# A chain of attention and two feed-forward layers: the second layer in three blocks of 768 tokens, its output product by Strassen's scheme too

## The chip, the core and the metric

The kernel runs on one core of one Trainium2 chip. The metric is the device time of one execution in microseconds (us); several executions are timed and their median is quoted.

## The reference, cut to what matters

```python
attn_out = _attn_ref(q, k, v, M_prev, z_prev, beta)        # B, H, S, D = 4, 8, 576, 64
x = attn_out.transpose(0, 2, 1, 3).reshape(2304, 512)
h = x @ w_in1;  r = np.maximum(h, 0.0)                     # 512 -> 2048
x = (s * (r * r) + b) @ w_out1                             # 2048 -> 512
h = x @ w_in2                                              # 512 -> 2048
sp = np.where(h > 20.0, h, np.log1p(np.exp(np.minimum(h, 20.0))))
out = (h * np.tanh(sp)) @ w_out2                           # 2048 -> 512
```

The weights arrive as 64-bit floats. The change is in the last three lines, "layer 2", and in how its weights are got ready.

## The kernel before

**Precision.** Every product is made of three fp32r products: an operand x is split into a high part (ScalarE copies it into an fp32r tile) and a low part (VectorE subtracts the high part from x), and high*high, low*high and high*low are added in PSUM. So each operand of a product costs a ScalarE copy and a VectorE subtraction, called a split below.

**Order.** The kernel is a list of steps with priorities. `Plan.order` runs them through a small model of the engines when the program is built and so fixes the order of the instructions on every engine; on the chip each engine runs its list in order, and semaphores hold back what isn't ready. A `Ring` is a set of buffer slots; `more(..., after=x)` adds slots that come free when step x is done.

**Layers.** Attention and layer 1 overlap. Layer 1 works on five blocks of 256 tokens and then two of 512 (`first`, `y_part`, `y_out`) and stores its result, transposed, in DRAM (`y_d`). Meanwhile `convert` turns the 64-bit weights into fp32: ScalarE, VectorE and one GpSimd addition (L656) for each of 32 pieces of 128x512 for layer 2, each then stored to DRAM (L670). The first pieces of layer 2 can go through once attention has left its buffers (`opened`).

**Layer 2.** Four blocks of 512 tokens and one of 256. `mish` makes one q of eight, that is 256 of the 2048 hidden columns: the input product is done by Strassen's scheme (in Winograd's form, seven products in place of eight) over two halves of the tokens, of the hidden columns and of the inner dimension; each product is six matmuls of 256 columns (L979). Three PSUM banks hold the results, VectorE adds them up (L985), ScalarE applies the activation (L989), and `finish` splits it (L935, L936). `load_y` makes the seven token-side operands of a block, `load_w` loads the weights of one q, forms their four sums on VectorE (L918) and splits them (L928, L929), anew for every block. `plain_pair` does the 256-token block without the scheme (L951). `o_part` is the output product in the plain form, 512 columns a matmul (L1014), put between the products of the next q. The split output weights stay in SBUF (`split_second`, once, L679 and L681). GpSimd has no work in layer 2.

## Time and profile before

| | |
|---|---|
| time, median of 3 runs | 1063.2 us (1062.54 to 1063.77) |
| the profiled execution, its own time | 1062.23 us |
| its span, first to last instruction | 1060.4 us |
| mean granted TensorE clock | 0.992 of full speed |
| attention with layer 1 | about 0 to 663 us of the span, its last products to 684 us |
| layer 2 | 663 to 1060 us |

PE is TensorE's matmuls, PEld its weight loads, DVE is VectorE, ACT ScalarE, POOL GpSimd; SPq is the queue from which SyncE issues DMAs. A matmul's bar is longer than its share of the time, since matmuls overlap; the pace is read from one start to the next.

### The profile page before, as it was taken

The numbers are of one execution on the slowest core, as the hardware profiler recorded it, in microseconds if no ns is written. First come the engines' busy times: TensorE is split into PE (matmuls) and PEld (weight loads), VectorE is DVE, ScalarE is ACT, GpSimd is POOL, SyncE is SP. The second block draws the span as 40 slices with busy tenths as digits, with TensorE's granted clock in tenths as the row PEclk, the third lists the DMA queues.
The fourth block names the chain that finished last, engine by engine and source line by source line (L and its number), as shares of the span: only waits on it lengthen the run. The fifth ranks groups of instructions, "written<-read, shape, count | busy, mean of one in ns | idle before, by whom it ended". The sixth has DMA issues, their size and how long they took to land.

```text
span 1060.4 us, 19441 instructions
## 1 busy us (share of the span) xinstructions
PE 1028.4 (97%) x6590; PEld 915.5 (86%) x6590; DVE 839.8 (79%) x2342; ACT 652.3 (62%) x1532; POOL 251.8 (24%) x337
## 2 busy tenths in 40 slices
PE   6989998999999999999989999999999999999998
PEld 4657787999999999999867888888899999999897
DVE  6899999999999999966797595796876977875432
ACT  6876897788888877865436553654453644553342
POOL 6854444343334334303224220000000000000000
PEclk9998998999999999999999999999999999999999
DMA  9663462323432423326546843331221221221220
GB/s 257 183 183 115 144 208 92 109 87 110 126 93 87 126 87 87 100 81 225 164 137 206 265 146 100 119 120 60 81 80 61 70 100 41 70 89 52 81 100 20
DMA packets 72051, 123.56 MB, mean 117 GB/s; under 512 B 7184, under 2 KB 48656, under 8 KB 71952
## 3 DMA queue, kind: packets, MB, share of 16 engines
q1 hardware_dynamic: 71520, 122.32, 37.5%
q8 instruction: 52, 0.85, 0.3%
q14 instruction: 47, 0.39, 0.1%
q10 hardware_dynamic: 432, 0.01, 0.0%
HBM read 99.75 MB, written 22.54 MB: 115 GB/s over the span
## 4 chain that ended last, share of the span: by engine, by line
PE 71%; DVE 14%; issue 4%; ACT 3%; DMA 3%; POOL 1%; DVEq 0%; ACTq 0%; POOLq 0%
PE o L1014 19%; PE h L723 12%; PE y L789 9%; PE h L979 9%; PE o L979 5%; PE a L567 4%; PE o L789 4%; PE a L539 3%; DVE total L693 2%; PE a L481 2%; PE h L951 1%; PE a L482 1%; DVE w L654 1%; PE o L723 1%; DVE Pt L486 1%
## 5 line engine op out<-in xcount | busy, mean ns | idle before, releaser
L656 POOL TENSOR_TENSOR w<-w,raw 128x512 int32<-128x512 int32 x54 | 75.7, 1402 | 166.9 <-DVE w L654 114.2
L498 POOL TENSOR_SCALAR Pt<-ex,nm 128x64 f32<-128x64 f32 x148 | 74.3, 515 | 85.4 <-PE a L539 45.7
L495 ACT ACTIVATE Pt<-Pt,mx 128x64 f32<-128x64 f32 (+4 forms) x148 | 81.8, 555 | 16.7 <-DVE mx L486 15.7
L539 PE MATMUL a<-ident,Pt 128*128 128x128 f32 x432 | 66.9, 281 | 9.1 <-POOL Pt L512 6.8
L547 DVE TENSOR_TENSOR PTl<-a,PTh 128x128 fp32r<-128x128 f32 (+1 forms) x144 | 64.0, 481 | 2.4 <-ACT PTh L544 1.6
L1014 PE MATMUL o<-woh,yh 128*128 128x512 f32 x232 | 63.4, 391 | 0.0
L1014 PE MATMUL o<-woh,gg 128*128 128x512 f32 x228 | 63.2, 394 | 0.0
L539 PEld LDWEIGHTS a<-ident,Pt 128*128 128x128 f32 x432 | 50.1, 143 | 14.5 <-POOL Pt L512 9.6
L486 DVE CUSTOM_DVE_ANT_0 Pt<-a,mask 128x320 f32<-128x320 f32 (+3 forms) x148 | 59.3, 417 | 3.3 <-PE a L482 1.5
L512 POOL TENSOR_SCALAR Pt<-Pt,rs 128x64 f32<-128x64 f32 x64 | 45.3, 755 | 64.3 <-DVE rs L517 50.9
L544 ACT CAST PTh<-a 128x128 fp32r<-128x128 f32 (+1 forms) x144 | 55.2, 431 | 3.3 <-PE a L539 2.4
L929 DVE TENSOR_TENSOR wil<-raw,wih 128x512 fp32r<-128x512 f32 (+2 forms) x69 | 52.3, 775 | 2.6 <-ACT wih L928 2.5
L789 PE MATMUL y<-gh,wol 128*128 128x256 f32 x320 | 54.0, 292 | 0.0
L789 PE MATMUL y<-gl,woh 128*128 128x256 f32 x320 | 53.5, 289 | 0.0
L789 PE MATMUL y<-gh,woh 128*128 128x256 f32 x320 | 53.0, 289 | 0.0
L989 ACT ACTIVATE g<-g 128x256 f32<-128x256 f32 (+1 forms) x42 | 21.9, 523 | 49.1 <-DVE g L985 48.9
L985 DVE TENSOR_TENSOR g<-o,g 128x256 f32<-128x256 f32 x58 | 24.5, 423 | 33.6 <-PE o L979 33.4
L567 PE MATMUL a<-PTl,V 128*128 128x384 f32 (+1 forms) x192 | 47.3, 293 | 1.6 <-DVE PTl L547 1.4
L567 PE MATMUL a<-PTh,V 128*128 128x384 f32 (+1 forms) x192 | 48.4, 280 | 0.0
L928 ACT CAST wih<-raw 128x512 fp32r<-128x512 f32 (+2 forms) x69 | 46.0, 687 | 2.7 <-DVE raw L918 1.3
L646 ACT ACTIVATE w<-raw 128x512 f32<-128x512 f32 x54 | 36.2, 671 | 17.4 <-DMA w_out_d<-w 8.8
L789 PEld LDWEIGHTS y<-gh,woh 128*128 128x128 f32 x320 | 45.4, 194 | 1.4 <-issue 0.7
(443 smaller groups left out, 3294.0 us busy)
## 6 DMA issues: line engine op xcount, KB each, us to landing
qk<-in_qk SPq DMA_DIRECT2D x24, 608.0 KB, 3.9
raw<-in_w_out SPq DMA_DIRECT2D x28, 512.0 KB, 3.9
raw<-w_in_d SPq DMA_DIRECT2D x28, 512.0 KB, 3.7
raw<-in_w_in SPq DMA_DIRECT2D x26, 512.0 KB, 4.6
wf<-w_in_d SPq DMA_DIRECT2D x12, 512.0 KB, 3.7
qn<-in_qz SPq DMA_DIRECT2D x29, 192.0 KB, 2.4
vx<-in_vm SPq DMA_DIRECT2D x29, 160.0 KB, 2.4
out<-ot SPq DMA_DIRECT2D x18, 256.0 KB, 2.1
```

Source lines behind the costliest of these rows:

```text
L486: nc.vector.tensor_tensor_reduce(Pt[t].t[:, D + lo:D + hi], ps.t[:, :hi - lo], mask[:, SP - w + lo:SP - w + hi], -SCALE, mx.t[:, t:t + 1] ...
L495: nc.scalar.activation(Pt[t].t[:, D:w + D], Pt[t].t[:, D:w + D], AF.Exp, bias=mx.t[:, t + i:t + i + 1], scale=-1.0, accum_out=rs.t[:, t:t ...
L498: add(POOL, 0.3, lambda: nc.gpsimd.tensor_scalar(Pt[t].t[:, :D], ex.t[:, t, :], nm.t[:, t:t + 1], 1.0, op0=ALU.mult, op1=ALU.mult), [ex, n ...
L539: nc.tensor.transpose(ps.t[:, c - c0, :], Pt[t].t[:, c * P:(c + 1) * P], ident)
L544: (nc.vector.tensor_copy if dve else nc.scalar.copy)(PT[0].t[:, at_], ps.t[:, :n])
L547: nc.vector.tensor_tensor(PT[1].t[:, at_], ps.t[:, :n], PT[0].t[:, at_].bitcast(F32), op=ALU.subtract)
L567: nc.tensor.matmul(o.rearrange("p (t q) -> p t q", q=P), v, x.t[:, f[0]:f[-1] + 1:f[1] - f[0] if len(f) > 1 else 1, :], start=(c == 0 and ...
L656: add(POOL, 1.23, prio, lambda: nc.gpsimd.tensor_tensor(w.t, w.t, words()[:, :, 0], op=ALU.add), [raw, low_words, w], [w])
L723: nc.tensor.matmul(ph, w_at(1, nm, r, cc)[:, o:o + P], x_at(x, cc), start=(part == 0 and cc == 0), stop=(part == 2 and cc == NCC - 1))
L789: nc.tensor.matmul(acc[ec // per].t[:, (ec % per) * n:(ec % per + 1) * n], w_at(1, nm, r, jj)[:, ec * P:(ec + 1) * P], t(x), start=(big an ...
L979: nc.tensor.matmul(ps.t[:, :h], w.t[:, i, kk], x.t[:, k, kk], start=begin and part == kk == 0, stop=part == 2 and kk == 1, skip_group_chec ...
L1014: nc.tensor.matmul(acc[i].t, gg.t[:, k, i * P:(i + 1) * P], W[2, nm, r][0].t[:, jj, :], start=(fc == 0 and part == 0), stop=(fc == NFC - 1 ...
```

## The change

Layer 2 takes three blocks of 768 tokens, all by Strassen's scheme. Each block runs in two phases. In the first (`hidden`, eight q), the input products are seven products of six matmuls with 384 columns; the four quarters of the activated result stay in SBUF as fp32 (`g2`), and VectorE forms three sums of them. In the second (`out_block`), the output product is done by the same scheme over halves of the tokens, the hidden columns and the output columns: seven products p of eight q, each 3 tiles of 128 tokens by 3 parts, in matmuls of 256 columns. Their token-side operands are split on the fly into a ring of eight slots (`S`), and VectorE adds the products into `p1`, `e2` and the output tile.

The sums of the weights are formed once, on GpSimd, while the weights are converted (`combine_in`, `combine_out`: four sums for each pair of pieces), and stored to DRAM with the pieces. Each block loads and splits the weights of each q and of each p anew. In the first block every second split weight tile (`kk`=1, `half`=1) is also stored split, and the later blocks load these tiles ready-made by a DMA issued from GpSimd's queue. The sums of the tokens' operands move from VectorE to GpSimd (`minus`), and so does one sum of the hidden quarters. PSUM is one pool of eight banks (`bk` in layer 2, three for a q or a p), and many buffers become parts of larger tiles (`Home`), whose homes are freed weights of layer 1. The ring `sc` for the sums and two more slots for converted pieces (`w32`) come free when layer 1's blocks of 256 tokens are done and stored (`small_left`).

```diff
-    N2 = 512
-    blocks2 = [(t, min(N2, NT - t)) for t in range(0, NT, N2)]
-    NB2 = len(blocks2)
+    N2 = 768
+    H2 = N2 // 2
+    NB2 = NT // N2
+    NQ2 = NFC // 2
+    DH = DM // 2
...
+    WID = [dram.tile([P, 2, 2, 7, P], F32, name=f"wi{r}_d") for r in range(NR)]
+    WOD = [dram.tile([P, 7, NQ2 // 2, DH], F32, name=f"wo{x}_d") for x in range(2)]
+    WIS = [dram.tile([P, 2, 7, P], F32R, name=f"wi_split{q}_d") for q in range(NQ2)]
+    WOS = [dram.tile([P, 2, NQ2 // 2, DH], F32R, name=f"wo_split{p}_d") for p in range(7)]
...
+    banks = [Bank(psum.tile([P, 512], F32, name=f"bank{i}")) for i in range(8)]
...
+        sums(prio, [sc, w0, w1], [lambda: (s_(0), a(1, 0), a(1, 1), ALU.add), lambda: (s_(1), s_(0), a(0, 0), ALU.subtract),
+                                  lambda: (s_(2), a(0, 0), a(1, 0), ALU.subtract), lambda: (s_(3), a(0, 1), s_(1), ALU.subtract)])
+        stored(w0, lambda: WID[r][:, :, kk, 0], lambda: a(0, 0), prio, landed)
+        stored(w1, lambda: WID[r][:, :, kk, 1:3], lambda: w1.t.bitcast(F32).rearrange("p (o i n) -> p o i n", o=2, i=2), prio, landed)
+        stored(sc, lambda: WID[r][:, :, kk, 3:7], lambda: sc.t, prio, landed)
+        wi_in[r, kk] = landed
...
+            s3 = minus(lambda t3=t3: t3.t, b22, b12, [y0, y1], [t3])
+            s1 = minus(b12, b12, b11, [y0], [], [s3])
+            p11 = piece("B11", b11, y0)
+            s2 = minus(b11, b22, b12, [y0, y1], [], [s1, *p11])
+            piece("T2", b11, y0, [s2])
+            piece("T1", b12, y0, [s1])
+            p21 = piece("B21", b21, y1)
+            piece("T3", lambda t3=t3: t3.t, t3)
+            piece("B22", b22, y1)
+            s4 = minus(b21, b21, b11, [y0, y1], [], [s2, *p21])
+            piece("T4", b21, y1, [s4])
...
+    def split(prio, t, src, r, after=(), done=()):
...
+        for x in t[1]:
+            n *= x
+        hi = add(ACT, act_us(n), prio, lambda: nc.scalar.copy(t[0](0), src()), r, [t[2], half], after)
+        lo = add(DVE, dve_us(n), prio, lambda: nc.vector.tensor_tensor(t[0](1), src(), t[0](0).bitcast(F32), op=ALU.subtract),
...
+    def load_wi(blk, q, kk):
+
+        w, prio = Buf(R["W"], [P, 2, 7, P], F32R), when(blk, 0, 0, q) - 8.0
+        if blk and kk:
+            add(POOL, 1.0, prio, lambda: nc.gpsimd.dma_start(w.t, WIS[q]), [wi_split[q]], [w]).lag = 3.0 + load_us(14 * P)
+            return w
+        wf = Buf(R["wf"], [P, 7, P])
+        add(DMA, load_us(7 * P), prio, lambda: nc.sync.dma_start(wf.t, WID[q // 2][:, q % 2, kk]), [wi_in[q // 2, kk]], [wf])
+        split(prio, (lambda x: w.t[:, x], [7, P], w), lambda: wf.t, [wf])
+        if kk:
+            wi_split[q] = Buf()
+            add(DMA, load_us(14 * P), prio, lambda: nc.sync.dma_start(WIS[q].bitcast(F32), w.t.bitcast(F32)), [w], [wi_split[q]])
...
+    def load_wo(blk, p, half):
...
+        if blk and half:
+            add(POOL, 1.0, prio, lambda: nc.gpsimd.dma_start(w.t, WOS[p]), [wo_split[p]], [w]).lag = 3.0 + load_us(8 * DH)
+            return w
...
+        product(a, 0, NAMES[0], True, False)
+        kept = add(ACT, act_us(H2), ew, lambda: nc.scalar.copy(g.t[:, A12], a.t[:, :H2]), [a], [g])
+        product(b, 4, NAMES[1], True, False)
+        e1 = plus(A21, b, A12, [kept])
+        product(c, 3, NAMES[2], True, False)
+        e2 = plus(A22, c, A12, [kept])
+        product(a, 1, NAMES[3], False, True, [kept])
+        m1 = act(A11, lambda: a.t[:, :H2], [a], [kept])
+        product(b, 5, NAMES[4], False, False, [e1])
+        c22 = plus(A22, b, A22, [e2])
+        product(c, 6, NAMES[5], False, True, [e2])
+        c12 = plus(A21, c, A21, [e1])
+        m2 = act(A21, lambda: g.t[:, A21], [], [c12])
+        product(b, 2, NAMES[6], False, True, [c22])
+        c21 = plus(A12, b, A12, [e1, e2])
+        m3 = act(slice(A12, A22 + 1), lambda: g.t[:, A12:A22 + 1], [], [c21, c22], 2 * H2)
+        need = when(blk, 1, 0, q) - 6.0
+        s = first_pieces[q] = Buf(R["S"], [P, 2, H2], F32R)
+        hi, lo = split(need, (lambda x: s.t[:, x], [H2], s), lambda: g.t[:, A11], [], [m1])
+
+        def more(o_, x, y_, op, after, prio):
+            return add(DVE, dve_us(H2), prio, lambda: nc.vector.tensor_tensor(g.t[:, o_], g.t[:, x], g.t[:, y_], op=op), [], [g], after)
+
+        s1 = more(X, A21, A22, ALU.add, [m2, m3], need + 9.0)
+        s3 = more(A21, A11, A21, ALU.subtract, [s1, m1], need + 9.0)
+        s2 = more(A11, X, A11, ALU.subtract, [s3, hi, lo], need + 9.0)
...
+                s = Buf(R["S"], [P, 2, H2], F32R)
+                made = split(when(blk, 1, p, q) - 5.0, (lambda x, s=s: s.t[:, x], [H2], s), lambda g=g: g.t[:, src], [], [ready[src]])
+                for x in made:
+                    hold[q].append(x)
+                if p == 1:
+                    ready[A12] = add(POOL, 1.2, when(blk, 1, p, q) - 4.0, lambda g=g: nc.gpsimd.tensor_tensor(
+                        g.t[:, A12], g.t[:, A12], g.t[:, A11], op=ALU.subtract), [], [g], [*made, ready[A11]])
...
+        def mm(q, t):
+            s, x = pieces[q], w[q // 4]
+            for part in range(3):
+                j, k = ((0, 0), (0, 1), (1, 0))[part]
+                nc.tensor.matmul(acc[t].t[:, :DH], s.t[:, j, t * P:(t + 1) * P], x.t[:, k, q % 4],
+                                 start=q == part == 0, stop=q == NQ2 - 1 and part == 2)
...
+                x, k = {1: (p1, "p1"), 2: (p1, "p1"), 3: (p1, "p1"), 4: (e2, "e2"), 5: (p1, "p1"), 6: (e2, "e2")}[p]
+                if ot is not None:
+                    last["o", t] = plus(t, ot, ps, x, [ps], [ot], [last[k, t]])
+                if p == 2 or p == 4:
+                    last["p1", t] = plus(t, p1, ps, p1, [ps], [], [last["p1", t], last["o", t]])
+                if p == 3:
+                    last["e2", t] = plus(t, e2, ps, p1, [ps], [], [last["p1", t]])
...
+    low = Home(m1t, "low", 3584)
+    R["w32"].homes(low, [2048, 2560], small_left)
+    R["sc"] = Ring("sc").homes(low, [0, 1024], small_left)
...
+    for r in range(NR):
+        for kk in range(2):
+            combine_in(CONV2, r, kk, *[converted_piece("in", r, j) for j in (kk, kk + 2)])
+    for q in range(NQ2):
+        combine_out(CONV2, q, *[converted_piece("out", q // 2, q % 2 * 2 + j) for j in range(2)])
     converted = add(NONE, 0.0, 0.0, lambda: None, after=plan.steps[n:])
...
+    for r in range(2):
+        R["yc"].homes(Home(wpool, f"wi{r}", 4096, F32R), [768 * i for i in range(5)], left[r])
...
+    for nm, after in (("woh1_0", out_left[1]), ("wol1_0", out_left[1]), ("woh0_0", y_left), ("wol0_0", y_left)):
+        R["W"].homes(Home(wpool, nm, 2048, F32R), [0], after)
...
+    R["wf"].homes(stage, [1024 * i for i in range(3)], converted)
+    for nm, after in (("wih3_0", left[3]), ("wil3_0", left[3]), ("woh2_0", out_left[2]), ("wol2_0", out_left[2]),
+                      ("woh3_0", closed), ("wol3_0", closed)):
+        R["g2"].homes(Home(wpool, nm, 2048), [0], after)
+    R["g2"].more(m2c, 2, closed)
+    R["S"].homes(Home(m2c, "S", 6144, F32R), [768 * i for i in range(8)], closed)
+    R["p1"].more(m1, 1, closed, ["xh_0"])
+    R["e2"].more(m1, 1, closed, ["xh_1"])
+    R["ot"].more(m1, 1, closed, ["xl_0"])
+    R["bk"].banks(banks[4:6], banks_left).banks(banks[:2], inputs_left).banks([*banks[2:4], *banks[6:]], closed)
...
+    for blk in range(NB2):
+        for q in range(NQ2):
+            hidden(blk, q, 2000.0 + 20.0 * blk + q, -1000.0)
+        if blk + 1 < NB2:
+            load_y(blk + 1, when(blk + 1, 0) - 10.0, "2")
+        out_block(blk, 2010.0 + 20.0 * blk)
```

## Rows read from the trace of the kernel before

**Rows 1.** Page, part 1: each engine's busy time.

```profile
PE 1028.4 (97%) x6590; PEld 915.5 (86%) x6590; DVE 839.8 (79%) x2342; ACT 652.3 (62%) x1532; POOL 251.8 (24%) x337
```

**Rows 2.** Windows: stretch, its length, busy time (instructions) by engine, clock, DMA share, GB/s.

```profile
core 0: us, PE busy (x) PEld busy (x) DVE busy (x) ACT busy (x) POOL busy (x), PEclk, DMA share, GB/s
...
510.00:560.00 50.00, 47.08 (x201) 36.95 (x200) 45.13 (x66) 20.62 (x35) 13.55 (x10) 1.00 0.49 142
560.00:630.00 70.00, 69.33 (x298) 55.52 (x297) 52.39 (x95) 39.17 (x71) 23.39 (x16) 1.00 0.65 203
630.00:663.00 33.00, 33.00 (x144) 26.69 (x143) 20.39 (x36) 13.15 (x22) 0.00 (x0) 1.00 0.39 124
...
684.00:692.00 8.00, 7.77 (x57) 7.25 (x58) 7.87 (x16) 6.83 (x14) 0.00 (x0) 1.00 0.64 211
692.00:1056.00 364.00, 364.00 (x2266) 327.86 (x2264) 242.84 (x498) 167.62 (x342) 0.00 (x0) 1.00 0.22 71
```

**Rows 3.** Chain that ended last, in layer 2: start us, us, what.

```profile
704.50 0.91 PE o L1014 x4
705.41 0.71 PE h L979 x6
706.12 0.93 PE o L1014 x4
...
769.08 1.44 PE h L979 x12
```

**Rows 4.** Timeline, TensorE: first matmuls of layer 2, and the last.

```profile
663.46 0.40 PE L979 MATMUL h<-wih0a,wih 128*128 128x256 f32 x2
...
1055.99 0.39 PE L1014 MATMUL o<-woh,gg 128*128 128x512 f32 x1
```

**Rows 5.** Windows of one line, L789, where layer 1 ends.

```profile
663.40:684.00 20.60, 13.29 (x49) 8.23 (x48) 1.00 0.35 103
```

**Rows 6.** Timeline, VectorE in layer 2: start us, us, engine, operation.

```profile
746.95 0.42 DVE L985 TENSOR_TENSOR w<-h,w 128x256 f32<-128x256 f32 x1 [0.36 <-PE h L979]
747.29 0.68 DVE L936 TENSOR_TENSOR gg<-g,gg 128x512 fp32r<-128x512 f32 x1
747.89 0.68 DVE L929 TENSOR_TENSOR wil<-raw,wih 128x512 fp32r<-128x512 f32 x1
748.49 0.48 DVE L844 TENSOR_SCALAR yr<-yr,bcs 128x512 f32<-128x512 f32 x1
748.88 0.42 DVE L929 TENSOR_TENSOR wil<-raw,wih 128x256 fp32r<-128x256 f32 x1
...
750.61 1.22 DVE L929 TENSOR_TENSOR wil<-wf,wih 128x1024 fp32r<-128x1024 f32 x1
751.74 0.42 DVE L918 TENSOR_TENSOR raw<-raw 128x256 f32<-128x256 f32 x1
```

**Rows 7.** Timeline, GpSimd, and then VectorE, in the same stretch.

```profile
619.30 1.56 POOL L656 TENSOR_TENSOR w<-w,raw 128x512 int32<-128x512 int32 x1 [0.77 <-ACT wil0b L887]
...
619.01 0.68 DVE L881 TENSOR_TENSOR wih0b<-tt,wih0b 128x512 fp32r<-128x512 f32 x1
619.61 1.80 DVE L881 TENSOR_TENSOR wil0a<-tt,wil0a 128x512 fp32r<-128x512 f32 x1
```

**Rows 8.** Tile w, conversion for layer 2: ns min/median/max, first to last start us.

```profile
L646 ACT ACTIVATE w<-raw x32: 646/672/681, 479.9 to 621.0; 128x512 f32<-128x512 f32 x32
L656 POOL TENSOR_TENSOR w<-w,raw x32: 1287/1414/1964, 481.9 to 625.9; 128x512 int32<-128x512 int32 x32
L670 SPq DMA_DIRECT2D w_out_d<-w x16: 319/320/320, 499.1 to 627.5; - x16
```

**Rows 9.** Tensor y_d: layer 1's stores of its 256-token blocks, columns as above.

```profile
L817 SPq DMA_DIRECT2D y_d<-ys x20: 319/326/1084, 192.3 to 505.3; - x20
```

**Rows 10.** DMA issues: tensors, queue, count, KB each, median us from issue to landing.

```profile
raw<-w_in_d SPq DMA_DIRECT2D x28, 512.0 KB, 3.7
...
w_in_d<-w SPq DMA_DIRECT2D x16, 256.0 KB, 3.1
...
wol<-in_w_out SPq DMA_DIRECT2D x1, 512.0 KB, 7.1
```

More of the change, by code (lines that the diff above doesn't have):

```diff
@@ L104, in make @@
         self.t = pool.tile(self.shape, self.dtype, tag=tag, name=tag)
-    def can_make(self):
-        return bool(self.ring.free) and (not self.ring.fifo or self.ring.queue[0] is self)
     def take(self):
@@ L112, in take, with stuck_at @@
             self.ring.queue.pop(0)
+def stuck_at(bufs):
+    for ring in {id(b.ring): b.ring for b in bufs}.values():
+        mine = [b for b in bufs if b.ring is ring]
+        if len(ring.free) < len(mine) or (ring.fifo and any(x is not y for x, y in zip(ring.queue, mine))):
+            return ring
+    return None
 class Step:
@@ L212, in order @@
                 got = heappop(ready[e])[2]
-                stuck = next((b.ring for b in got.new if not b.can_make()), None)
+                stuck = stuck_at(got.new)
                 if stuck is not None:
@@ new lines, in convert, with load_us, stored, sums @@
+                [w, half], [W[lo, r]])
+        return w
+    def load_us(n):
+        return n * 512 / 310e3
+    def stored(w, dest, src, prio, landed):
+        add(DMA, load_us(256), prio, lambda: nc.sync.dma_start(dest(), src()), [w], [landed]).lag = 1.5
+    def sums(prio, out, table):
+        for f in table:
+            def one(f=f):
+                o_, x, y, op = f()
+                nc.gpsimd.tensor_tensor(o_, x, y, op=op)
+            add(POOL, 0.95, prio, one, out[1:], out[:1])
+    def combine_in(prio, r, kk, w0, w1):
+        sc, landed = Buf(R["sc"], [P, 2, 4, P]), Buf()
+        def a(i, j):
+            return (w0, w1)[j].t.bitcast(F32).rearrange("p (o i n) -> p o i n", o=2, i=2)[:, :, i]
+        def s_(i):
+            return sc.t[:, :, i]
+        sums(prio, [sc, w0, w1], [lambda: (s_(0), a(1, 0), a(1, 1), ALU.add), lambda: (s_(1), s_(0), a(0, 0), ALU.subtract),
[4 more added lines that the diff above has]
+        wi_in[r, kk] = landed
@@ new lines, in load_wo @@
+    def load_wo(blk, p, half):
+        w, prio = Buf(R["W"], [P, 2, NQ2 // 2, DH], F32R), when(blk, 1, p, 4 * half) - 8.0
+        slot = (0, 1, 4, 5, 3, 2, 6)[p]
+        if blk and half:
+            add(POOL, 1.0, prio, lambda: nc.gpsimd.dma_start(w.t, WOS[p]), [wo_split[p]], [w]).lag = 3.0 + load_us(8 * DH)
+            return w
+        wf = Buf(R["wf"], [P, NQ2 // 2, DH])
+        add(DMA, load_us(4 * DH), prio, lambda: nc.sync.dma_start(wf.t, WOD[half][:, slot]), [wo_in[4 * half + x] for x in range(4)], [wf])
+        split(prio, (lambda x: w.t[:, x], [4, DH], w), lambda: wf.t, [wf])
+        if half:
+            wo_split[p] = Buf()
+            add(DMA, load_us(8 * DH), prio, lambda: nc.sync.dma_start(WOS[p].bitcast(F32), w.t.bitcast(F32)), [w], [wo_split[p]])
+        return w
@@ L1027, in o_out @@
[L1027 to L1033 removed]
+            return add(PE, 6 * mm_us(H2), prio, mm, [*w, *x] + [ps] * (not begin), [ps], after)
@@ L1064, in attention_then_two_ffn @@
             j, fc = seq[i]
+            begin = len(plan.steps)
             if fc == 0:
@@ L1139, in zero_product @@
-        nc.tensor.matmul(idle[0][:, :256].rearrange("p (k n) -> p k n", n=P), zeros,
+        nc.tensor.matmul(banks[3].held[:, :256].rearrange("p (k n) -> p k n", n=P), zeros,
                          zeros.unsqueeze(1).to_broadcast([P, 2, P]), start=True, stop=True)
```

482 lines of the change are left out of this document (208 added, 274 removed).

## The prediction

> **What bounds the kernel now.** I read the page's busy times first: TensorE is busy for 97% of the span, VectorE for 79% [rows 1]. The windows by stage say where that matters: from 692 to 1056 us, which is layer 2, TensorE is busy 364.00 of 364 us at the full clock (2.4 GHz), while VectorE has 242.84 us (67%), ScalarE 167.62 (46%), the DMA engines 22% at 71 GB/s and GpSimd nothing [rows 2]. The chain of waits is an unbroken row of matmuls there [rows 3]. So layer 2 is bound by TensorE's instruction stream, and a matmul column less is time saved, for as long as the others keep up.
>
> **Prices.** In the chain, starts lie 0.91 us apart for four matmuls of 512 columns and 0.71 for six of 256; where only 256-column ones follow each other, 12 take 1.44 [rows 3]. With 0.92 for the four (the neighbouring steps range to 0.93) I take 0.23 us for 512 columns and 0.118 to 0.12 for 256. No 384-column stretch stands in the rows; half-way between its neighbours is 0.174.
>
> **What is removed and added on TensorE.** Before: four blocks of 8 q x 7 products x 6 = 1344 matmuls of 256 columns, 192 more in the last block, 18 token tiles x 16 x 3 = 864 of 512: 1536 x 0.118 + 864 x 0.23 = 380 us. The timeline agrees: layer 2 starts at 663.46, its last matmul at 1055.99 [rows 4], and of the 392.8 us up to 1056.2 some 11.1 are the 48 matmuls that L789 still has there (a 49th in that row starts before) [rows 5]: 381 with the gaps. After: 3 x 8 x 7 x 6 = 1008 of 384 columns and 3 x 7 x 8 x 9 = 1512 of 256: 175.4 + 178.4 to 181.4 = 354 to 357. **The removal is worth 23 to 27 us; I take 25.** With no new wait at all the profiled execution, 1062.2 us, would become 1037.2. The end hardly changes: one tile is still read out of PSUM and stored (half as wide, under 0.5 us less).
>
> **What may give part of it back.** Five places; for each a lower and an upper end.
>
> *VectorE in layer 2.* Starts lie 0.34 us apart for 256 columns (PSUM input or not), 0.60 for 512, 1.13 for 1024, 0.39 for the 512-column bias addition [rows 6]; between them, 384 columns cost 0.47, 896 cost 1.00, a bias of 768 about 0.53. First phase of a block, per q: five PSUM additions and three sums 8 x 0.47, one split 0.47, two weight splits 2.00 (one, 1.00, in later blocks): 6.2 or 5.2, for 8 q 50 or 42 us. Second phase: 48 splits 22.6, 14 weight splits 15.8 (later 7 for 7.9), 21 PSUM additions 7.1: 45.5 or 37.6. The next block's tokens: 14 splits and 4 biases, 8.7. So 104, 88 and 79 us for the three blocks, against 118.6 us of TensorE each: 88%, 74% and 67%. ScalarE does one copy for each split and the activations, on the same shapes but without the additions, so it stays below VectorE. DMA in the first block: 16 loads of 0.46 MB and 8 stores of 0.92, 14 loads of 0.52 and 7 stores of 1.05, tokens and output 3.1: 32.5 MB in 118.6 us, 274 GB/s; layer 2's 71 GB/s at a share of 0.22 means 323 at a full share [rows 2], so 85%. Full, but not over.
>
> *GpSimd against VectorE.* Layer 2 has GpSimd work again: per block eight sums of hidden quarters and eight of the next tokens (none in the last). What that does to VectorE shows where both work before layer 2: the same 512-column subtraction takes 0.68 us, and 1.80 when L656 starts on GpSimd 0.31 us ahead of it [rows 7]. A blocked subtraction loses 1.1 us. If all 16 of the first block hit one, VectorE has 104 + 18 = 122 us for a block of 118.6. Cost in the first block: 0 to 5 us; I take 2, since PSUM additions and ScalarE's part of a split leave gaps. The Trainium skill states the mechanism in "SBUF — State Buffer", section "Who interferes with whom": a VectorE instruction with two SBUF inputs and a GpSimd instruction that reads SBUF exclude each other for a whole instruction. The trace agrees (1.80 against 0.68). By that rule every one of the 16 can cost VectorE its full length, the term is 5 instead of 2 and the sum below 1049.
>
> *Short chains in the first phase.* In `hidden` one bank takes two or three products in turn, and the later one waits until VectorE has read the earlier. Before, output products stood between; now only the next q's products can. The nearest row is the stretch 684 to 692, where only such products ran: TensorE busy 7.77 of 8 us [rows 2], 3% idle. On 3 x 58.5 us that is 5; products of 1.04 us instead of 0.72 and eight banks leave more slack. 0 to 5; I take 2.
>
> *Conversion and layer 1's end.* Now 32 pieces go through from 479.9 to 628, about 4.6 us each [rows 8], and `wf` opens when all are stored. After, the first pair holds its two slots until `sc` opens, which is when layer 1's small blocks have been stored: 505.3 [rows 9] plus a landing, say 508. Fifteen pairs follow. GpSimd alone needs 2 x 1.41 [rows 8] + 4 x 0.75 (half of the 512-column addition, rounded up) = 5.8 us a pair; two pieces at the present rate and the sums, with nothing overlapped, 12.2. With two pairs in flight I take 7.5: finished near 628, first weights loaded (3.7 [rows 10]) and split by 640, in time for 663.5, when layer 1 has 11 us of matmuls left as cover. If not, TensorE has matmuls until about 663.5 + 11 = 675. At 12.2 a pair the first weights come at 508 + 7 (the first pair's sums and stores) + 183 + 8 = 706: cost 0 to 31 us; I take 1. On the way VectorE gets less room: TensorE idles 2.9 us of 510 to 560 with VectorE 90% busy [rows 2], and GpSimd's 64 sums block it more. If the same 5.8% idles in all of 510 to 663, that is 6 more; if the idle goes, 3 less. I take 2.
>
> *Weights issued from GpSimd's queue.* In the second and third block the second tile of a q (0.92 MB) is loaded by a DMA that GpSimd issues once the tile of two q earlier is free. Its time from free slot to landed, L, is in no row. SyncE's 0.5 MB land in 3.7 us, at worst 7.1 [rows 10]; 0.4 MB more at 323 GB/s make 5.0 to 8.4, and one sum ahead in GpSimd's queue up to 1.3 more: L is 5 to 9.7. A q uses its tile for 7.3 us plus d, at most one foreign product (1.04) before its last one; two tiles in turn give each q (7.3 + d + L)/2, so the wait is (L + d - 7.3)/2 for 14 q: nothing to 24 us. With L near 7, in the middle, and a d that shows half the time, I take 2. In the output phase a tile has half a p more, 4.3 us, and waits for none of this. What queues behind such an issue is GpSimd's own sums, needed four products later.
>
> **Sum.** 1062.2 - 25 + (2 + 2 + 1 + 2 + 2) = 1046. The median of the runs shown is 1.0 us above the profiled execution, so 1047.
>
> **Rivals.** (1) *VectorE becomes the bound*, held up by GpSimd's instructions: first block + 5, chains + 5, layer 1's end + 6, and the rest as above: 1037.2 + 16 + 3 = 1056, 1057 on the median. For it: 1.80 against 0.68, and 88% in the first block; against it: later blocks have a quarter of VectorE free. (2) *The GpSimd-issued loads decide*: at L + d = 10.7 the 14 q lose 24 us, 1068. Slower than before needs L + d above 9.6 (16 us more than the 2 in the sum). For it: nothing in the trace shows that queue, and landings of 7 us exist; against it: 7.1 is one DMA, and 28 of 0.5 MB have a median of 3.7 [rows 10]. The Trainium skill's "DMA: Bandwidth & Descriptors" (section "Anatomy of one DMA") gives 2.0 us plus bytes at 436 GB/s for a DMA of that queue; an estimate from it is 4.1 us, by which no q waits and the sum would be 1044. No run here shows it yet. (3) *Conversion is late*: TensorE idles from 675 until the first weights. The gain is gone when they come at 692 (16 us over the 1 in the sum), at 11.3 us a pair; at 12 the end is 1073. For it: six GpSimd instructions a pair instead of two, and stores behind them; against it: four slots instead of two, and today's 4.6 us a piece is mostly the two slots waiting for stores (3.1 us each [rows 10]). (4) *All cover holds*: 1037 to 1040.
>
> **Chances.** Forecast (1040 to 1052) 0.58, (4) 0.06, (1) 0.17, (2) 0.12, (3) 0.07. This measurement can tell about 0.2%, 2.1 us. Faster: the forecast, (4), nearly all of (1): 0.79; within: 0.05, from (2) and (3) near their turning points; slower 0.16, the rest of these. The range takes the forecast, (4), (1) and the lower part of (2) and (3): 1037 to 1068; the forecast alone is 1040 to 1052.
>
> **What would show it.** TensorE in layer 2 with 1008 matmuls at 0.174 us and 1512 at 0.12; if 384 columns cost more than 0.176, the removal is mis-sized. Gaps of TensorE: in first phases before T3 or T4 with VectorE as releaser (chains), at the first matmul of a q with a GpSimd-queue DMA as releaser (rival 2), between 675 and 700 with a weight split as releaser (rival 3). VectorE at 90% or more in the first block, with subtractions over 1 us beside GpSimd's (rival 1). First weights split by 640. The prediction is wrong if the gaps of layer 2 come to more than 20 us, or to less than 2.

## Result and the profile after

The changed kernel takes 1070.2 us in the median of 12 runs (1063.5 to 1072.7), the kernel before 1062.7 us in 12 runs beside it: a ratio of 1.0063, with a 95% interval of 1.0047 to 1.0080. It is slower by 0.6%; 1047 us was forecast, and slower had a chance of 0.16.

The page's busy times of the changed kernel's profiled execution (own time 1071.3 us, span 1069.5 us), beside [rows 1]:

```profile
PE 1014.9 (95%) x6710; PEld 933.9 (87%) x6710; DVE 908.9 (85%) x2294; ACT 665.4 (62%) x1518; POOL 392.9 (37%) x479
```

TensorE's busy time went down by 13.5 us, but its share fell from 97% to 95%, and VectorE's rose from 79% to 85%. GpSimd has 393 us of work instead of 252. Where that falls show the windows by stage, with the columns of [rows 2]; the last one runs from the first product of layer 2 to the start of the last:

```profile
510.00:560.00 50.00, 43.61 (x178) 34.50 (x177) 49.13 (x60) 19.01 (x33) 29.54 (x25) 0.93 0.44 142
560.00:630.00 70.00, 67.55 (x282) 53.63 (x282) 59.14 (x77) 34.17 (x60) 56.26 (x52) 0.98 0.77 251
630.00:663.00 33.00, 30.15 (x119) 23.96 (x118) 31.14 (x36) 16.40 (x33) 25.92 (x22) 0.90 0.48 160
680.80:1066.20 385.40, 372.33 (x2569) 367.08 (x2567) 312.39 (x519) 202.09 (x362) 68.74 (x70) 0.98 0.61 205
```

In 510 to 560 us TensorE lost 3.5 us more than before and the clock fell to a mean of 0.93 between its levels of 2.4 and 1.2 GHz; in 630 to 663 it had been busy throughout and at full clock and now idles 2.9 us at 0.90. VectorE is full there (49.13 of 50 and 31.14 of 33 us, before 45.13 and 20.39). The first product of layer 2 starts at 680.8 us instead of 663.46 [rows 4]: **17.3 us are lost before layer 2.** From the first product to the start of the last, layer 2 takes 385.4 us instead of 392.5. A gain of 25 was forecast; 7 are there, and 13.1 of the 385.4 us are idle time of TensorE.

Who released TensorE, by the view of its waits from 475 us on (instruction that waited, releaser, total, times, longest):

```profile
PE bank L812 <- DVE g L858: 11.3, 4, 6.0
PE bank L1088 <- DVE S L935: 10.4, 6, 2.9
PE bank L1022 <- DMA wol<-wi_split_d: 2.2, 2, 1.2
...
PE bank L1022 <- DVE g L1028: 0.2, 1, 0.2
```

All that is long waits for VectorE: layer 1's activation in the first row, the splits of the output phases in the second. The weight loads from GpSimd's queue cost 2.2 us.

**What VectorE does meanwhile.** In its groups by line between 510 and 663 us (the last number before the second bar is the mean of one in ns) a 512-column subtraction (L861) takes 1.08 us; before it took 0.69. The conversion's L704 takes 0.80 instead of 0.49. L858, which reads PSUM and one SBUF tile, takes what it always took:

```profile
line engine op names shapes xcount | busy us, mean ns | idle before us <-releasers
L858 DVE SCALAR_TENSOR_TENSOR g<-bank,g 128x512 f32<-128x512 f32 x24 | 16.3, 681 | 4.0 <-ACT g L857 4.0
L861 DVE TENSOR_TENSOR xh<-g,xh 128x512 fp32r<-128x512 f32 x15 | 16.2, 1082 | 4.0 <-ACT xh L860 3.8
...
L704 DVE TENSOR_SCALAR low<-low 128x512 int32<-128x512 int32 x16 | 12.7, 802 | 0.5 <-ACT low L697 0.5
```

The timeline shows one such place. GpSimd's four sums of one weight pair (L732) run without a break from 541.27, and the next three VectorE instructions take 1.1 to 1.2 us each. Layer 1's activation (L858) stands behind them in VectorE's fixed order. TensorE waits 5.96 us for it; the three instructions account for some 1.5 us of that (3.52 us against three times 0.68), the rest is what VectorE was behind already. The two groups of four matmuls after the wait take 2.08 and 1.91 us, at a granted clock of 0.50 from 545.8 to 549.5 us (the lower level), where a few us later four take 1.07.

```profile
541.27 4.45 POOL L732 TENSOR_TENSOR low<-low 128x256 f32<-128x256 f32 x4
541.67 1.21 DVE L861 TENSOR_TENSOR xh<-g,xh 128x512 fp32r<-128x512 f32 x1
...
542.80 1.21 DVE L782 TENSOR_TENSOR total<-total,woh 128x512 f32<-128x512 f32 x1
544.04 1.10 DVE L782 TENSOR_TENSOR total<-total,wol 128x512 f32<-128x512 f32 x1
545.06 0.68 DVE L858 SCALAR_TENSOR_TENSOR g<-bank,g 128x512 f32<-128x512 f32 x1
...
545.79 2.08 PE L812 MATMUL bank<-yh,wih 128*128 128x512 f32 x4 [5.96 <-DVE g L858]
...
547.67 1.91 PE L878 MATMUL bank<-xl,wol 128*128 128x512 f32 x4
...
552.63 1.07 PE L878 MATMUL bank<-xh,woh 128*128 128x512 f32 x4
```

In the second phase of block one the same happens with L1080 (a hidden quarter's subtraction on GpSimd). The VectorE instructions that start with or behind one take 1.36 to 1.37 us, the free ones 0.55, and TensorE waits 2.84 us for the split (767.17) that its next matmul needs. Seven matmuls then go through in 1.10 us; the nine after them take 2.01 us, at a granted clock of 0.53 from 768.7 to 770.7, where a few us earlier eighteen took 2.28:

```profile
762.41 2.28 PE L1088 MATMUL bank<-wol,S 128*128 128x256 f32 x18
...
763.66 0.55 DVE L935 TENSOR_TENSOR S<-g,S 128x384 fp32r<-128x384 f32 x1
763.82 1.27 POOL L1080 TENSOR_TENSOR wol<-wol 128x384 f32<-128x384 f32 x1 [1.63 <-DVE S L935]
...
764.13 1.37 DVE L1055 TENSOR_TENSOR g<-g 128x384 f32<-128x384 f32 x1
...
767.17 0.55 DVE L935 TENSOR_TENSOR S<-wih,S 128x384 fp32r<-128x384 f32 x1
767.39 1.19 POOL L1080 TENSOR_TENSOR g<-g 128x384 f32<-128x384 f32 x1 [1.02 <-DVE g L1055]
767.63 1.36 DVE L935 TENSOR_TENSOR wi<-low,wi 128x384 fp32r<-128x384 f32 x1
...
767.77 1.10 PE L1088 MATMUL bank<-woh,S 128*128 128x256 f32 x7 [2.84 <-DVE S L935]
...
768.70 2.01 PE L1088 MATMUL bank<-wol,S 128*128 128x256 f32 x9
```

Windows of 20 us, one from each of the first two blocks, show what a block's mean hides: VectorE is busy for 20.00 of 20 us, in block two as well (an instruction that is held up counts as busy).

```profile
760.00:780.00 20.00, 15.09 (x108) 14.44 (x108) 20.00 (x26) 10.57 (x21) 10.31 (x9) 0.89 0.60 193
...
880.00:900.00 20.00, 17.01 (x136) 16.61 (x135) 20.00 (x24) 12.08 (x25) 14.68 (x13) 0.96 0.33 109
```

### The profile page after: what moved, and what is told of

It reads as the page before. It is cut to its first block, busy times and chain, and to the rows that moved or that the text cites. A ratio compares the mean times of both kernels' runs of the same rounds, so it can differ in the third digit from the quotient of the medians.

```text
span 1069.5 us, 20053 instructions
## 1 busy us (share of the span) xinstructions
PE 1014.9 (95%) x6710; PEld 933.9 (87%) x6710; DVE 908.9 (85%) x2294; ACT 665.4 (62%) x1518; POOL 392.9 (37%) x479
## 4 chain that ended last, share of the span: by engine, by line
PE 62%; DVE 20%; issue 6%; DMA 4%; ACT 3%; POOL 2%; SPq 0%; DVEq 0%; ACTq 0%; POOLq 0%
PE bank L1022 16%; PE bank L878 12%; PE bank L1088 12%; PE bank L812 11%; PE bank L626 4%; PE bank L598 3%; DVE total L782 2%; DVE S L935 2%; PE bank L540 1%; DVE PTl L606 1%; PE bank L541 1%; DVE stage L705 1%; DVE wi L935 1%; DMA wol<-wi_split_d 1%; DVE Pt L545 1%
## 5 line engine op out<-in xcount | busy, mean ns | idle before, releaser
L1088 PE MATMUL bank<-woh,S 128*128 128x256 f32 x792 | 107.4, 285 | 6.2 <-DVE S L935 6.1
L1022 PE MATMUL bank<-wi,woh 128*128 128x384 f32 x384 | 113.1, 335 | 0.0
L1088 PEld LDWEIGHTS bank<-woh,S 128*128 128x128 f32 x792 | 100.7, 193 | 7.0 <-DVE S L935 6.7
L1088 PE MATMUL bank<-wol,S 128*128 128x256 f32 x720 | 99.6, 287 | 4.5 <-DVE S L935 4.3
L1022 PE MATMUL bank<-wi,wol 128*128 128x384 f32 x336 | 97.4, 335 | 2.2 <-DMA wol<-wi_split_d 2.2
L1088 PEld LDWEIGHTS bank<-wol,S 128*128 128x128 f32 x720 | 92.4, 194 | 5.8 <-DVE S L935 5.1
L598 PE MATMUL bank<-ident,Pt 128*128 128x128 f32 x432 | 66.7, 281 | 10.3 <-POOL Pt L571 7.8
L1022 PEld LDWEIGHTS bank<-wi,woh 128*128 128x128 f32 x384 | 70.7, 188 | 0.8 <-DVE wih L1028 0.2
L606 DVE TENSOR_TENSOR PTl<-bank,PTh 128x128 fp32r<-128x128 f32 (+1 forms) x144 | 63.9, 481 | 2.4 <-ACT PTh L603 1.7
L1022 PEld LDWEIGHTS bank<-wi,wol 128*128 128x128 f32 x336 | 61.7, 188 | 3.0 <-DMA wol<-wi_split_d 2.7
```

The source lines that it names most:

```text
L598: nc.tensor.transpose(ps.t[:, c - c0, :], Pt[t].t[:, c * P:(c + 1) * P], ident)
L606: nc.vector.tensor_tensor(PT[1].t[:, at_], ps.t[:, :n], PT[0].t[:, at_].bitcast(F32), op=ALU.subtract)
L1022: nc.tensor.matmul(ps.t[:, :H2], w[kk].t[:, j, i], x[kk].t[:, k], start=begin and part == kk == 0, stop=part == 2 and kk == 1, skip_group_ ...
L1088: nc.tensor.matmul(acc[t].t[:, :DH], s.t[:, j, t * P:(t + 1) * P], x.t[:, k, q % 4], start=q == part == 0, stop=q == NQ2 - 1 and part == 2)
```

## Experiments

Theory 1: a GpSimd instruction that reads SBUF holds VectorE's instruction up (and the other way round), and where VectorE is full this reaches TensorE. Theory 2: VectorE merely has too much work of its own in these stretches. Theory 3: GpSimd's own slow, dependent instructions are late. Times are medians; ratios are to the kernel before, run beside each. "First" and "last" are the starts of layer 2's first and last product in the profiled execution, "length" lies between them.

| kernel | time, us | ratio (95%) | first | last | length |
|---|---|---|---|---|---|
| before | 1062.7 | | 663.5 | 1056.0 | 392.5 |
| after | 1070.2 | 1.0063 (1.0047 to 1.0080) | 680.8 | 1066.2 | 385.4 |
| e1 sums on VectorE | 1070.9 | 1.0078 (1.0047 to 1.0109) | 680.6 | 1063.4 | 382.8 |
| e2 quarters on VectorE | 1046.5 | 0.9841 (0.9811 to 0.9872) | 672.2 | 1038.4 | 366.2 |
| e3 both | 1047.6 | 0.9855 (0.9827 to 0.9882) | 676.6 | 1042.2 | 365.6 |
| e4 sums as writes | 1057.4 | 0.9957 (0.9938 to 0.9976) | 669.4 | 1054.2 | 384.8 |
| e5 quarters as writes | 1044.7 | 0.9822 (0.9806 to 0.9839) | 675.2 | 1041.1 | 365.9 |
| e6 token quarters on VectorE | 1063.2 | 0.9999 (0.9989 to 1.0009) | 673.0 | 1055.7 | 382.7 |
| e7 hidden quarters on VectorE | 1064.0 | 1.0004 (0.9987 to 1.0021) | 679.4 | 1057.6 | 378.2 |
| e8 = e2, column sums on TensorE | 1040.9 | 0.9789 (0.9773 to 0.9805) | 671.7 | 1036.1 | 364.4 |
| e9 before, token sums on GpSimd | 1063.1 | 1.0001 (0.9990 to 1.0012) | | | |
| e10 before, weight sums too | 1064.9 | 1.0019 (1.0003 to 1.0035) | | | |
| e11 before, column sums on TensorE | 1063.7 | 1.0015 (1.0002 to 1.0027) | | | |
| e12 column sums on TensorE | 1061.4 | 0.9987 (0.9966 to 1.0009) | 670.9 | 1055.5 | 384.6 |
| e13 sums and quarters as writes | 1037.4 | 0.9761 (0.9726 to 0.9795) | 664.2 | 1029.7 | 365.5 |
| e14 token quarters as writes | 1054.9 | 0.9929 (0.9904 to 0.9954) | 673.0 | 1048.7 | 375.7 |
| e15 hidden quarters as writes | 1054.2 | 0.9920 (0.9893 to 0.9946) | 681.0 | 1052.5 | 371.5 |

**GpSimd's work moved to VectorE (e1, e2, e3).** The edit of e1, and that of e2, which also does it to the subtraction at L1080:

```diff
-                nc.gpsimd.tensor_tensor(o_, x, y, op=op)
-            add(POOL, 0.95, prio, one, out[1:], out[:1])
+                nc.vector.tensor_tensor(o_, x, y, op=op)
+            add(DVE, dve_us(256), prio, one, out[1:], out[:1])
...
-            return add(POOL, 1.2, prio, lambda: nc.gpsimd.tensor_tensor(o_(), x(), y(), op=ALU.subtract), r, w, after, keep)
+            return add(DVE, dve_us(H2), prio, lambda: nc.vector.tensor_tensor(o_(), x(), y(), op=ALU.subtract), r, w, after, keep)
```

e1: 

> The 64 sums of weight quarters in the conversion run on VectorE instead of GpSimd. Theory 1 (a GpSimd instruction that reads SBUF holds VectorE up): VectorE gets 64 additions of about 0.4 us (26 us) but loses the stretching beside 64 GpSimd additions of about 0.97 us, which is about as much; layer 1's last output product stays near 704 us or comes a few us earlier, 1062 to 1071 us. Theory 2 (VectorE simply has too much of its own between 510 and 663 us): the 26 us come on top of a VectorE that is full, layer 1 ends near 720 us, 1080 us or more. Theory 3 (GpSimd's chain in the conversion is too slow): the conversions end earlier and layer 2 starts earlier, 1055 to 1062.

e2: 

> The eight subtractions of token quarters and the eight of hidden quarters in each block run on VectorE instead of GpSimd. Theory 1: the TensorE waits of some 13 us in the second phases of blocks one and two shrink to 6 or less, and the clock lost behind them comes back, 1058 to 1066 us. Theory 2 (load of VectorE): 16 instructions of 0.55 us are added to each of the first two blocks, waits stay or grow, 1070 to 1080.

e3: 

> Both moves together, so that GpSimd reads SBUF in layer 2 not at all and in layer 1 only for the conversions' integer additions. Theory 1: the sum of the two, 1052 to 1066 us. Theory 2: 1085 or more.

e1 changed nothing that can be told (1070.9): 64 additions on VectorE cost as much there as 64 GpSimd reads beside it, which theory 1 said and theory 2 put at 1080 or more. e2 gave 24 us, more than theory 1 had expected; theory 2 fell for layer 2, since VectorE got more work and the kernel became faster. Moving the quarters shortened layer 2 to 366.2 us and brought its start forward by 8.6. e3 shows again that the sums are a tie; with 1047.6 us it, too, came out below what theory 1 had for it (1052 to 1066).

**The same order, without the reads (e4, e5).** Moving work changes the order of the list. Here the list, its costs and GpSimd's busy time stay, and only what GpSimd executes is replaced; layer 2 computes with other numbers. The edit of e4; e5 does the same to the quarters:

```diff
-                nc.gpsimd.tensor_tensor(o_, x, y, op=op)
+                for _ in range(3):
+                    nc.gpsimd.memset(o_, 0.01)
```

e4: 

> The 64 sums are replaced by three writes of a constant each on GpSimd, at the same place of the same order, which write SBUF and read nothing (layer 2 then computes with other weights). Theory 1: VectorE's stretched instructions between 510 and 663 us go back to near 0.7 us except beside the conversions' integer additions, layer 1 ends 10 us earlier or more, 1054 to 1062 us. Theory 2 and theory 3 (GpSimd is as long busy as before): 1068 to 1072.

e5: 

> The GpSimd subtractions of token and hidden quarters are replaced by three writes of a constant each, at the same place of the same order; they write SBUF and read nothing, and keep GpSimd about as long (layer 2 then computes with other quarters). Theory 1 (GpSimd's reads hold VectorE up): nearly the gain of the move to VectorE, 1045 to 1052 us. Theory 3 (what costs is GpSimd's own length, about 1.3 us for each of a chain of dependent subtractions): 1062 to 1070.

Three writes keep GpSimd as long as the read did. The rows of GpSimd's groups for L1080, in the changed kernel and in e5 (three writes of 420 ns make 1.26 us, against 1.40):

```profile
L1080 POOL TENSOR_TENSOR wol<-wol 128x384 f32<-128x384 f32 x6 | 8.4, 1400 | 3.1 <-DVE S L935 3.1
```

```profile
L1080 POOL MEMSET wol<- 128x384 f32 x18 | 7.6, 420 | 0.7
```

e4's windows show layer 1's end with 6.1 us more of matmuls in 510 to 663 us (147.4 against 141.3) than that of the changed kernel; layer 2 starts at 669.4, 11.4 us earlier:

```profile
510.00:560.00 50.00, 47.59 (x204) 37.70 (x203) 47.20 (x67) 19.89 (x35) 32.07 (x69) 1.00 0.50 161
560.00:630.00 70.00, 69.21 (x297) 55.44 (x296) 53.00 (x79) 39.16 (x69) 57.45 (x125) 1.00 0.86 276
630.00:663.00 33.00, 30.62 (x131) 24.17 (x130) 25.66 (x32) 14.06 (x28) 22.60 (x38) 1.00 0.42 140
```

In e5 the waits for `S` in the second phases are gone from the list of TensorE's waits; what is left stands in layer 1, and two loads:

```profile
PE bank L812 <- DVE g L858: 8.9, 3, 6.0
PE bank L1022 <- DMA wol<-wi_split_d: 2.6, 2, 1.5
```

Layer 2 of e5 has the same 519 VectorE instructions in the same order as that of the changed kernel. They take 284.11 us instead of 312.39, and TensorE's clock is 1.00:

```profile
675.20:1041.10 365.90, 363.32 (x2569) 360.70 (x2567) 284.11 (x519) 201.66 (x362) 64.58 (x147) 1.00 0.65 217
```

The instructions that got shorter are those with two SBUF inputs: the `wi` splits and the sums of `g`. First the groups of the changed kernel, then those of e5:

```profile
L935 DVE TENSOR_TENSOR wi<-low,wi 128x384 fp32r<-128x384 f32 x20 | 16.8, 848 | 0.0
...
L1055 DVE TENSOR_TENSOR g<-g 128x384 f32<-128x384 f32 x18 | 14.8, 823 | 0.0
```

```profile
L935 DVE TENSOR_TENSOR wi<-low,wi 128x384 fp32r<-128x384 f32 x20 | 10.8, 550 | 0.0
...
L1055 DVE TENSOR_TENSOR g<-g 128x384 f32<-128x384 f32 x18 | 9.9, 551 | 0.0
```

The other way round shows too: in the changed kernel GpSimd's 256-column sums (L732) take 0.73 us at the quickest and 0.99 in the mean.

Theory 3 fell with e4 and e5: GpSimd is busy as long, but the loss in layer 2 is gone in e5, and two thirds of the loss ahead of it in e4. The Trainium skill says what the runs show: "SBUF — State Buffer", section "Who interferes with whom", has VectorE instructions with two SBUF inputs contend with a GpSimd instruction that reads SBUF, and not with one that only writes it. The runs agree with both halves, 0.85 us beside reads against 0.55 beside writes for the `wi` splits; no 384-column split of e5's layer 2 takes more than 0.56.

**Do the parts add up? (e13, e14, e15)** Writes in place of all that was added on GpSimd, of the token quarters alone, and of the hidden ones alone.

e13: 

> All GpSimd reads that the change added (64 sums of weight quarters, the token and the hidden quarters) are replaced by three constant writes each, the order unchanged (layer 2 computes with other numbers). If the parts add up: layer 2's first product near 664 us (680.8 less 11.4 and 5.6), its length 366 us, 1033 to 1038 us. If the parts hide each other: 1040 to 1045.

e14: 

> Only the token quarters' reads are replaced by writes, the order unchanged. If each held-up VectorE instruction costs for itself: layer 2 starts near 675 us and takes about 376 us, half-way between 385.4 and 365.9: 1054 to 1058 us. If the move of one kind alone brought little because of the hidden quarters' reads that stay: a length of 380 to 385, 1059 to 1065.

e15: 

> Only the hidden quarters' reads are replaced by writes, the order unchanged; layer 2 starts as late as in the changed kernel. Half of the loss in layer 2: about 1060 us. If the token quarters' reads that stay do most of it by themselves: 1065 to 1070.

They do at layer 1's end, as far as single executions can tell: 680.8 less 11.4 (e4) and 5.6 (e5) is 663.8, and e13 measured 664.2, within a microsecond of the kernel before. That it fits so closely is luck: by 510 us, before the first of these reads, 3492 matmuls had started in the changed kernel, 3488 in e4 and 3499 in e13, which at 0.23 us each is a spread of some 2.5 us. e13's layer 2 has VectorE at 284 us and TensorE idle for 2.5, and with 1037.4 us it is the fourth rival of the prediction, all cover holding:

```profile
664.20:1029.70 365.50, 362.96 (x2569) 360.26 (x2568) 284.01 (x519) 201.58 (x362) 64.51 (x147) 1.00 0.65 217
```

The windows of the three blocks, each from its first input product, show where the 19.9 us between the changed kernel (above) and e13 (below) lie: 11.4, 7.9 and 0.6. Blocks one and two hold 18 and 14 of the 40 reads; block three has eight, and VectorE a quarter of its time free:

```profile
680.80:820.50 139.70, 134.51 (x889) 131.16 (x888) 121.95 (x193) 79.48 (x138) 24.09 (x19) 0.96 0.72 241
820.50:947.20 126.70, 120.01 (x842) 118.75 (x842) 100.92 (x170) 65.06 (x120) 26.38 (x29) 0.99 0.58 192
947.20:1066.20 119.00, 117.81 (x842) 117.17 (x841) 89.52 (x156) 57.55 (x104) 18.27 (x22) 1.00 0.53 178
```

```profile
664.20:792.50 128.30, 128.30 (x889) 126.12 (x889) 109.78 (x193) 79.18 (x138) 22.63 (x52) 1.00 0.78 263
792.50:911.30 118.80, 117.41 (x843) 117.14 (x842) 90.29 (x170) 64.85 (x120) 24.93 (x57) 1.00 0.62 206
911.30:1029.70 118.40, 117.25 (x842) 116.99 (x840) 83.94 (x156) 57.55 (x104) 16.95 (x38) 1.00 0.53 178
```

Even without the reads VectorE is full for 20 us in block one and nearly so in block two, and TensorE waits for nothing there:

```profile
765.00:785.00 20.00, 20.00 (x173) 20.00 (x173) 20.00 (x40) 14.27 (x25) 2.83 (x5) 1.00 0.75 270
846.00:866.00 20.00, 20.00 (x155) 20.00 (x154) 19.34 (x37) 15.93 (x33) 12.90 (x32) 1.00 0.53 184
```

In layer 2 the two kinds of quarters cost 9.7 (e14) and 13.9 us (e15) when taken away singly, and 19.5 to 19.9 together (e5, e13), so they overlap a little. Both singly brought what separate costs give, e15 more than the 1060 us expected of it (its profiled execution, 1057.7 us, is the highest of its runs).

**One kind moved (e6, e7).** The edit of e2 for one of the two kinds.

e6: 

> Only the eight subtractions of token quarters in each block move to VectorE; the hidden ones stay on GpSimd. Layer 2's first product comes near 672 us instead of 681, and the waits in the second phases shrink in part. Theory 1 with the costs shared by both kinds: 1052 to 1058 us. If the token quarters alone are the cause: 1045 to 1049.

e7: 

> Only the eight subtractions of hidden quarters in each block move to VectorE; the token ones stay on GpSimd. Layer 2 starts as late as in the changed kernel. Costs shared by both kinds: 1058 to 1064 us; if the token quarters alone are the cause, 1068 to 1071.

Both brought 6 to 7 us only, where e2 brought 24; e6 missed the 1052 to 1058 us that theory 1 had for it. Set beside e14 and e15, where the same reads are gone but VectorE has no more work and the old order, layer 2 is 7 us longer in both (382.7 against 375.7, 378.2 against 371.5). Without any reads the moved work costs nothing (366.2 against 365.9). In both, 5.7 of the 7 us are more idle time of TensorE (14.3 against 8.6, 10.7 against 5.0), and part of that is a longer wait at the start of block two, for the first weights from GpSimd's queue. From issue to landing the first two of these loads take 7.9 to 9.2 us here, 5.9 to 6.4 in e14 and e15, whose waits for such loads come to 2.3 and 1.0 us. The lists of waits of e6 and of e7 have:

```profile
PE bank L1022 <- DMA wol<-wi_split_d: 4.1, 1, 4.1
```

```profile
PE bank L1022 <- DMA woh<-wi_split_d: 5.1, 2, 4.9
```

Whether the rest is VectorE's added 0.47 us at each place or the new order beside the reads that stay, no run separates, nor why these loads take longer.

**VectorE's own load at layer 1's end (e8, e11, e12).** The 31 additions of the column sums (L782) become 32 matmuls with ones in the changed kernel (e12), in e2 (e8) and in the kernel before (e11):

```diff
-                add(DVE, dve_us(512) * (2 if r + j else 1), prio, pair, [W["woh", r], W["wol", r]] + [total] * (r + j > 0), [total],
-                    after=[begin] * (r + j == 0))
...
-        add(PE, 0.87, prio, lambda: nc.tensor.matmul(ps.t, ones.t, total.t, start=True, stop=True), [ones, total], [ps])
+        def columns():
+            for i, (r, j, nm) in enumerate((r, j, nm) for r in range(NR) for j in range(FPR) for nm in ("woh", "wol")):
+                nc.tensor.matmul(ps.t, ones.t, w_at(nm, r, j), start=i == 0, stop=i == 2 * NR * FPR - 1)
+        add(PE, 32 * 0.23, prio, columns, [ones] + [W[nm, r] for r in range(NR) for nm in ("woh", "wol")], [ps])
```

e8: 

> Token and hidden quarters on VectorE, and the 31 VectorE additions of the column sums are replaced by 32 matmuls with ones (7.4 us on TensorE in place of 0.9; about 28 us less on VectorE between 510 and 630 us). If VectorE's load is what is left of the lateness of layer 1's end (690.6 against 682.9 us): that end comes near 682 us or earlier and the time is 1034 to 1042 us. If it is the blocking beside the conversions' GpSimd additions, or the conversions themselves: 1046 to 1054.

e11: 

> In the kernel before, the column sums become 32 matmuls with ones, so that the gain of the same move in the changed kernel can be set beside it. VectorE is no bound of layer 1 here but for the 2.9 us that TensorE idles between 510 and 560 us; TensorE gets 6.5 us more: 1063 to 1068 us. If layer 1's end is held up by VectorE here too: 1058 to 1062.

e12: 

> The changed kernel with the column sums on TensorE alone; all GpSimd reads stay where they are. If layer 1's end is late because VectorE is full (its own work and the blocking together), layer 2 starts 8 to 14 us earlier: 1055 to 1062 us, with the waits of the second phases unchanged. If it is late for another reason: 1070 to 1077.

e12 starts layer 2 at 670.9, 9.9 us earlier although TensorE has some 6.5 us more to do (by the costs in the list), and leaves its length as it was (384.6). So layer 1's end is late because VectorE is full, and taking away either its own work or GpSimd's reads helps. e8 is the fastest kernel with the full computation, 1040.9 us, as expected, but layer 1's end did not come near 682 us: its last product starts at 695.1, in e2 at 696.5. At 510 us e8's execution was 16 matmuls behind e2's (3483 against 3499), some 3.7 us; from there to layer 2's first product TensorE idles 1.4 us in e8 and 9.7 in e2. It idles 1.1 us in e8's layer 2:

```profile
671.70:1036.10 364.40, 363.32 (x2569) 360.25 (x2567) 297.38 (x553) 200.97 (x361) 16.15 (x30) 1.00 0.63 209
```

In the kernel before the same move brings nothing (e11), so e8's gain of 22 us is the change's, with the quarters' reads taken out and the weight sums still on GpSimd.

**The other way round, in the kernel before (e9, e10).** Its token sums (e9), then also the four weight sums of each q (e10), move from VectorE to GpSimd, 40 reads a block:

```diff
-            nc.vector.tensor_tensor(t[x], a0, a1, op=ALU.subtract)
+            nc.gpsimd.tensor_tensor(t[x], a0, a1, op=ALU.subtract)
```

e9: 

> The other way round: in the kernel before, the subtractions of token quarters (8 of 256 columns in each full block) move from VectorE to GpSimd. If a GpSimd read costs time wherever it stands (the 48 reads of the changed kernel cost some 29 us, 0.6 each): 32 of them, 1075 to 1085 us. If it costs only where VectorE is full, and a third of VectorE's time is free here: 1061 to 1065.

e10: 

> In the kernel before, the sums of weight quarters in layer 2 (four for each q of each full block, 256 columns) move to GpSimd as well, 40 reads a block. A fixed price of 0.6 us a read: 1140 us or more. A price only where VectorE is full: VectorE is relieved of 40 additions of 0.42 us a block and held up about as long, 1062 to 1070 us; more only if the sums' longer chain on GpSimd makes weights late, which would show as waits for a weight split.

e9 costs nothing that can be told, e10 2.0 us (0.3 to 3.7). VectorE's instructions are held up here too; the groups of the kernel before and then of e10 have a 512-column split at 0.69 and 0.92 us:

```profile
L936 DVE TENSOR_TENSOR gg<-g,gg 128x512 fp32r<-128x512 f32 x16 | 10.8, 687 | 1.7 <-ACT gg L935 1.7
```

```profile
L936 DVE TENSOR_TENSOR gg<-g,gg 128x512 fp32r<-128x512 f32 x16 | 14.5, 916 | 1.7 <-ACT gg L935 1.7
```

But the window of layer 2 in e10 has 132 GpSimd instructions, VectorE at 217 of 358 us, and TensorE busy for all but 1.7 (the move also takes the additions off VectorE, which had 242.84 of 364 us before, and e10 does not separate the two):

```profile
692.00:1050.00 358.00, 356.29 (x2223) 320.77 (x2222) 217.31 (x364) 165.76 (x338) 129.31 (x132) 1.00 0.22 73
```

A GpSimd read has no price of its own: it costs where the instruction it holds up, or one behind it, is the next that TensorE waits for.

## Why the prediction was wrong

**The removal was right, and a little small.** Without the reads layer 2 takes 365.5 us (e13) instead of 392.5: 27.0 where 25 (23 to 27) was taken, and 2.5 us of waiting for loads are still in it. In e13 matmuls of 384 columns start 0.173 us apart and those of 256 columns 0.117, where 0.174 and 0.118 to 0.12 were taken.

**The step that failed is "GpSimd against VectorE", and with it the part for VectorE's room in "Conversion and layer 1's end"; the mechanism was right and its size was not.** In layer 2 the term was 2 us (0 to 5); it measures 19.9 (385.4 against 365.5). At layer 1's end it was 2 us (at most 6); it measures 16.6 (680.8 against 664.2), of which the weight sums are 11.4 and the first block's token quarters 5.6. Four microseconds stood for 36.5; by the medians of the changed kernel and e13 it is 32.9, since the profiled execution is above the median in one and below it in the other. Three things made it small:

- VectorE was averaged over a whole block (88%, 74%, 67%), and only the first block was thought full. The averages were right (86%, 76% and 71% in e13), but the work of the second phases' beginning comes in a burst with the next block's tokens, and in such 20 us VectorE is full in block two too, with the reads (20.00) and nearly so without them (19.34). So the first block lost 11.4 us instead of at most 5, and the second 7.9 instead of nothing. There was little slack to hold the 0.7 us of VectorE's time that each of the 40 reads in layer 2 cost (28.3 us by the difference of 312.39 and 284.11).
- A wait was counted as its length alone. In layer 2, 10.5 of the 19.9 us are idle time (13.1 against 2.5 us), and the other 9.4 are more busy time for the same matmuls (372.33 against 362.96), at a granted clock of 0.85 to 0.96 in the 20-us windows around the waits in blocks one and two.
- For layer 1's end the 5.8% of idle time between 510 and 560 us was extended to 663. The reads added to it instead: they lengthen VectorE's queue, and the conversions, the column sums and the splits of the first tokens stand in it one behind the other.

**The other terms.** Short chains (2): TensorE's waits for L1028 in the first phases are 0.2 us; nothing. Conversion late (1): its pace was wrong, and it cost next to nothing. The last of its sums end at 668.6 us instead of near 628 (9.9 us a pair from 510.4, where 7.5 was taken; without the reads, in e13, still at 653.0), and the first weights are split from 676.9 on, not by 640. But TensorE has layer 1's products until then: it is busy for all of 663 to 680.8 us, no wait for a first weight split stands in the list above, and e13's start, 0.7 us after that of before, leaves the term that at most. Loads from GpSimd's queue (2): 2.2 us in the changed kernel, 2.5 in e13. From issue to landing, which no row of before showed, they take about the lower end of the 5 to 9.7 us assumed (the page's DMA issues, KB each, median us; 7.8 at the longest):

```profile
wol<-wi_split_d POOLq DMA_DIRECT2D x12, 896.0 KB, 4.9
```

The Trainium skill's "DMA: Bandwidth & Descriptors" (section "Anatomy of one DMA") had given 4.1 us as an estimate; the measured 4.9 decides, and in the changed kernel no q waits long by either.

**The rivals.** The first, VectorE as the bound, is what happened. At 1056 us it had 16 us for all that VectorE might cost, so it ended on the wrong side of 1062 too. The second and third didn't happen. (The second's turning point has a slip that changes nothing: 16 us more than the 2 in the sum are 18 for 14 q, so L + d above 9.9, not 9.6.) The fourth, 1037 to 1040 us, is what the change gives without the added GpSimd reads: 1037.4 in e13, which doesn't do that work at all. With all of that work on VectorE it is 1047.6 (e3); with the quarters alone moved, 1046.5, and 1040.9 with the column sums on TensorE as well (e2, e8). That e2 is at the forecast of 1047 is a coincidence of another sum: its give-back lies at layer 1's end.

The text's test for itself, gaps in layer 2 above 20 us, would not have shown the error: the gaps came to 13.1 us, since slower matmuls took 9.4 more and nearly half of the loss lies ahead of layer 2. Of the two signs it named for the first rival, subtractions over 1 us beside GpSimd's showed it; VectorE at 90% or more in the first block did not (121.95 of 139.7 us, 87%), although VectorE was what TensorE waited for.
